# Attention loads and stores in paced pieces of about 256 KB

## The chip, the cores and the metric

The kernel runs on one core of a Trainium2 chip. The metric is the device time of one execution in microseconds; a profiled execution also gives a span from its first to its last instruction. The engines named below are TensorE (PE, with its weight loads as PEld), VectorE (DVE), ScalarE (ACT), GpSimd (POOL) and SyncE (SP), which here only issues DMAs, in the order of its queue.

## What is computed

Attention over 8 batches and 8 heads, 512 local and 32 global positions with 64 channels, then a mixture of experts on its output. Cut to what matters:

```python
s_g = scale * np.matmul(q_g, k_all.transpose(0, 1, 3, 2))        # 32 global queries see all keys
out_g = np.matmul(sm(s_g), v_all)
mask = np.abs(pos[:, None] - pos[None, :]) <= 32                 # local queries: a window and the global keys
a_l = sm(np.concatenate([s_lg, np.where(mask, s_ll, -1e9)], axis=-1))
out_l = np.matmul(a_l, np.concatenate([v_g, v_l], axis=2))
x = concat([out_g, out_l]).transpose(0, 2, 1, 3).reshape(4608, 512)
logits = x @ w_gate                                              # greedy assignment, 576 tokens to each expert
out[assigned == e] = np.maximum(x[assigned == e] @ w1[e], 0.0) @ w2[e]
```

## The kernel before

Attention runs as 40 steps, five for each batch: four local ones, each for a pair of heads (`Local`), and one for the 32 global queries of all heads (`Glob`). In the last batch the global step comes second. Tile `qk` holds the transposed queries and keys of a pair (704 KB), `vw` its values in an even and an odd arrangement: the even half comes by DMA (520 KB), the odd half by four GpSimd copies from it (`load_v`). Seven buffers of each rotate.

The order is written by hand. In loop turn i, TensorE computes the scores S of step i+2 (L169, or L248 and L256 for a global step), transposes the probabilities of step i (T, L132 or L205), and computes the outputs O of step i-1 (L143, or L223 for a global step, which reads the vw tiles of all four pairs). Transposes and small matmuls for the gate (L274, L280, L289) of earlier batches follow. VectorE masks (L122) and normalises (L149 to L154), ScalarE takes the exponential (L127) and moves T into SBUF (L266). After the last local step of a batch its output tile `xs` (1 MB) is stored to `xd` in one DMA (L157); a global step stores eight pieces of 8 KB from `xg` (L235). Routing and the experts' stage (from about 240 us) come after.

All these DMAs stand in SP's queue. At the head of a turn the loop issues loads up to four pairs ahead of the pair whose scores are due, qk in two DMAs (L75, L76) and vw in two (L84). A DMA into a buffer waits until its last readers are done, and each DMA on SP waits for the eighth before it to have landed (eight semaphores in turn); whatever stands behind it in the queue waits too.

Of the kernel before, what the change touches and what calls it, by code (L numbers as in the profile page):

```python
# [63 lines left out]
def attention(ctx, tc, A, consts, xd, ident, L, nbatch, rt=None):  # L64
# [5 lines left out]

    qk, vw, xs = {}, {}, {}

    def load_qk(b, p):
        t = ld.tile([128, QW + KW], F32, name="qk", bufs=7)
        nc.sync.dma_start(t[:, :QW], A["qk"][b, p, :, :QW])  # L75
        nc.sync.dma_start(t[:, QW:], A["qk"][b, p, :, QW:])  # L76
        qk[b, p] = t

    def load_v(b, p):
        t = ld.tile([128, 2, 2, NW // 2, D + 1], F32, name="vw", bufs=7)  # L80
        ev, od = t[:, 0], t[:, 1]
        n = NW // 2
        for h in range(2):
            nc.sync.dma_start(ev[:, h].rearrange("p w d -> p (w d)"), A["vw"][b, p, :, h * n * (D + 1):(h + 1) * n * (D + 1)])  # L84
        nc.gpsimd.tensor_copy(od[0:64], ev[64:128])  # L85
        nc.gpsimd.tensor_copy(od[64:96], ev[32:64])
        nc.gpsimd.tensor_copy(od[96:128, :, :n - 1], ev[64:96, :, 1:])
        nc.gpsimd.tensor_copy(od[96:128, :, n - 1:], ev[64:96, :, n - 1:])
        vw[b, p] = t
# [6 lines left out]
    load_qk(0, 0)  # L96
    nc.sync.dma_start(mask.rearrange("p a b -> p (a b)"), A["mask"])
    nc.sync.dma_start(ident, A["ident"])
    load_qk(0, 1)
    load_v(0, 0)  # L100
    nc.sync.dma_start(wg.rearrange("p a b -> p (a b)"), A["wg"])
    load_qk(0, 2)
    load_v(0, 1)
    nl = [3]
    warm = ac.tile([128, 128], F32, name="warm")
    nc.vector.memset(warm, 0.0)
    wt = ps.tile([128, NB, 128], F32, name="T", bufs=3)
    for _ in range(WARM):
        nc.tensor.matmul(wt[:, 0, :], warm, warm, start=True, stop=True)
    for i in range(3):  # L110
        nc.gpsimd.memset(pg[i], 0.0)

    class Local:
# [15 lines left out]
        def turn(s):  # L129
            s.t = ps.tile([128, NB, 128], F32, name="T", bufs=3)  # L130
            for c in range(NB):
                nc.tensor.transpose(s.t[:, c, :], s.p[:, c, :], ident)  # L132

        def take(s):
            s.pt = wk.tile([128, NB, 128], F32, name="pt", bufs=5)
# [2 lines left out]
        def out(s):  # L138
            b, q, h = s.b, s.q, s.h
            s.o = ps.tile([128, NB, D + 1], F32, name="O", bufs=2)  # L140
            for c in range(NB):
                for r in range(4):
                    nc.tensor.matmul(s.o[32 * r:32 * r + 32, c, :], s.pt[:, c, 32 * r:32 * r + 32],  # L143
                                     vw[b, q][:, r % 2, h, 2 * c + r // 2, :], start=True, stop=True)

        def norm(s):
            b, q, h, o = s.b, s.q, s.h, s.o
            ls = wk.tile([128, NB], F32, name="ls", bufs=4)
            nc.vector.tensor_scalar(ls, o[:, :, D], 1e-9, None, op0=ALU.add)  # L149
            nc.vector.reciprocal(ls, ls)  # L150
            if q + h == 0:
                xs[b] = wk.tile([128, NB, DM], F32, name="xs", bufs=2)
            hd = 2 * q + h
            nc.vector.tensor_tensor(xs[b][:, :, 64 * hd:64 * hd + 64], o[:, :, 0:D],  # L154
                                    ls[:, :, None].to_broadcast([128, NB, D]), op=ALU.mult)
            if q == NP - 1 and h == 1:
                nc.sync.dma_start(ap_of(xd, (b * S + SG) * DM, [[DM, 128], [128 * DM, NB], [1, DM]]), xs[b])  # L157

    def local_scores(u):
        t = qk[u[0].b, u[0].q]  # L160
        for x in u:
            x.st = ps.tile([128, NB, 128], F32, name="S", bufs=3)
        for c in range(NB):
            for r in range(4):
                j = 4 * c + r
                k0 = QW + 32 * ((3 * j + 1) // 2)
                for h in range(2):
                    e = slice(64 * h, 64 * h + 64)
                    nc.tensor.matmul(u[h].st[32 * r:32 * r + 32, c, :], t[e, 32 * j:32 * j + 32], t[e, k0:k0 + 128],  # L169
                                     start=True, stop=True)  # L170

    class Glob:
# [27 lines left out]
        def turn(s):  # L200
            s.t = []
            for lo, n in ((0, 4), (4, 2)):
                t = ps.tile([128, NB, 128], F32, name="T", bufs=3)
                for k in range(n):
                    nc.tensor.transpose(t[:, k, :], s.p[:, lo + k, :], ident)  # L205
                s.t.append(t)
                s.part(lo, n)

# [8 lines left out]
        def out(s):  # L217
            b, h = s.b, s.h
            s.o = ps.tile([128, D], F32, name="O", bufs=2)
            for k in range(6):  # L220
                for r in range(4):
                    j = 3 * k + 1 if k < 5 else 14
                    nc.tensor.matmul(s.o[32 * r:32 * r + 32, :], s.pt[:, k, 32 * r:32 * r + 32],  # L223
                                     vw[b, r][:, j % 2, h, j // 2, 0:D],
                                     start=(k == 0), stop=(k == 5))

# [11 lines left out]
    def glob_scores(u):  # L238
        b = u[0].b
        for x in u:  # L240
            x.sa = ps.tile([128, 512], F32, name="S", bufs=3)
        for x, n, k in zip(u, "ST", (3, 3)):
            x.sb = ps.tile([128, 32], F32, name=n, bufs=k)

        def small(h):
            for r in range(4):
                e = slice(64 * h, 64 * h + 64)
                nc.tensor.matmul(u[h].sb[32 * r:32 * r + 32], qk[b, r][e, SL:SL + SG], qk[b, r][e, QW + 32:QW + 64],  # L248
                                 start=True, stop=True)
        small(0)  # L250
        for r in range(4):
            for h in range(2):
                t = qk[b, r]
                e = slice(64 * h, 64 * h + 64)
                base = t[e, QW + 64:QW + 128]
                nc.tensor.matmul(u[h].sa[32 * r:32 * r + 32].rearrange("p (a b) -> p a b", b=64), t[e, SL:SL + SG],  # L256
                                 ap_of(base, 0, [list(base.ap[0]), [96, 8], [1, 64]]), start=True, stop=True)
        small(1)

# [10 lines left out]
    def gate_x(src, xt, c, spare):  # L270
        t = ps.tile([128, NB, 128], F32, name="S" if spare else "T", bufs=3 if spare else 3)
        n = src.shape[1]
        for k in range(n):
            nc.tensor.transpose(t[:, k, :], src[:, k, c * 128:(c + 1) * 128], ident)  # L274
        evac(xt[:, c, :n * 128], t[:, :n].rearrange("p a b -> p (a b)"), "x")

    def gate_m(xt, n):
        lt = ps.tile([128, 512], F32, name="T", bufs=3)
        for c in range(4):
            nc.tensor.matmul(lt[32 * c:32 * c + 32, :n * 128], wg[:, c, :], xt[:, c, :n * 128],  # L280
                             start=True, stop=True)
        ltc = wk.tile([128, 512], F32, name="ltc", bufs=2)
        evac(ltc[:, :n * 128], lt[:, :n * 128], "l")
        return ltc

    def gate_l(ltc, J, n):
        t = ps.tile([128, NB, 4, 32], F32, name="T", bufs=3)
        for k in range(n):
            nc.tensor.transpose(t[:, k].rearrange("p a b -> p (a b)"), ltc[:, k * 128:(k + 1) * 128], ident)  # L289
# [36 lines left out]
    for b in range(nbatch):  # L326
# [11 lines left out]
        else:  # L338
# [5 lines left out]
            if gl:  # L344
# [3 lines left out]
                put(s0 + 9, 0, gl[4])  # L348
                put(s0 + 10, 0, gl[5])

    first = rt.setup(slice(0, 28)) if rt else None
    LA = 2
    for i in range(-LA, ns + 1):
        if rt and i == 1:
            rt.load()
# [15 lines left out]
        if cur:  # L371
            cur[0].turn()
        if cur:
            cur[0].take()
        if cur:
            cur[1].turn()
        if cur:
            cur[1].take()
        if nx:
            nx[0].mask()  # L380
        if nx:
# [4 lines left out]
            nx[1].exp()  # L386
        if old:
            old[0].out()
        if old:
            old[0].norm()  # L390
        if old:
            old[1].out()
        if old:
            old[1].norm()
        for f in extra.get((i, 0), []):
            f()
        for f in extra.get((i, 1), []):
            f()
        for f in extra.get((i, 2), []):
            f()  # L400
        if rt and i >= ns - 1:
            for _ in range(12):
                next(first, None)
# [649 lines left out]
```

## Time and profile before

| | us |
|---|---|
| median of 3 runs (740.04 to 744.93) | 743.16 |
| the profiled execution | 743.98 |
| its span | 742.2 |
| attention and gate, to the last L289 | about 240 |
| share of the 16 DMA engines, 18 to 197 us, in SP's queue | 65.6% |

The rows of the profile are read so. A row of waits names the engine and line that was idle, what released it, the sum, the count and the longest in us. "issue" stands for a time in which the engine waited for no other engine and no DMA that the profile shows. A row of a window gives its bounds, its length, each engine's busy time with the number of instructions, the clock granted to TensorE (1.00 is full), the mean busy share of the DMA engines and GB/s. A row of the timeline gives start, length, engine, line, operation, tiles and count, with the idle time before it in brackets. DMA queue rows give the queue and kind, packets, MB and share of the 16 engines.

### The profile page before, as it was taken

What the parts mean: (1) busy time and instruction counts of PE and PEld (TensorE: products, weight loads), DVE (VectorE), ACT (ScalarE), POOL (GpSimd) and SP (SyncE); (2) the same over time, 40 slices, a digit from 0 to 9 for tenths busy, and PEclk for the clock granted to TensorE, in tenths of its full rate; (3) what the DMA queues carried; (4) which work ended last, traced back from release to release, by engine and by line L of the source; (5) the groups of instructions that cost most, each with busy time, mean ns of one, the idle gap of its engine ahead of it and who ended that gap; (6) DMA issues with size and microseconds to landing.
All of it is one profiled execution on the core that took longest, in us unless ns stands there. A gap on an engine that the chain in (4) does not pass through costs nothing.

```text
span 742.2 us, 23504 instructions
## 1 busy us (share of the span) xinstructions
PE 667.9 (90%) x9824; PEld 543.8 (73%) x9824; DVE 480.3 (65%) x1762; ACT 320.1 (43%) x867; POOL 220.2 (30%) x247
## 2 busy tenths in 40 slices
PE   7788889888697259999999999999999999999997
PEld 6566657666474159778878978978877987988985
DVE  3586767677576788867676777775876865551410
ACT  5676766767481024334334334343342423541420
POOL 4833553553520040052043034034024025312002
PEclk8999999999898569999999999999999999999999
DMA  9665864876622052081072063044035044522001
GB/s 343 262 210 169 293 223 152 284 256 185 221 93 76 1 181 108 1 284 65 2 263 85 2 241 108 2 165 169 16 128 206 17 172 155 195 68 94 15 15 46
DMA packets 37034, 103.36 MB, mean 139 GB/s; under 512 B 7232, under 2 KB 7488, under 8 KB 32832
## 3 DMA queue, kind: packets, MB, share of 16 engines
q0 software_dynamic: 10240, 51.39, 19.8%
q1 hardware_dynamic: 26688, 50.48, 19.7%
q8 instruction: 77, 1.26, 0.7%
q14 instruction: 29, 0.24, 0.1%
HBM read 84.02 MB, written 17.83 MB: 137 GB/s over the span
## 4 chain that ended last, share of the span: by engine, by line
PE 77%; DVE 10%; issue 6%; DMA 4%; ACT 2%; SPq 0%; POOLq 0%; POOL 0%; DVEq 0%; ACTq 0%
PE Y L931 22%; PE H L903 21%; PE S L169 6%; PE T L132 5%; PE O L143 4%; PE R L513 4%; PE H L775 2%; DVE r_G L445 2%; PE T L274 2%; DVE w2l L445 2%; PE T L205 2%; PE Y L921 2%; PE O L223 2%; DMA qk<-in_qk_dram 1%; PE T L280 1%
## 5 line engine op out<-in xcount | busy, mean ns | idle before, releaser
L903 PE MATMUL H<-xh,w1h 128*128 128x272 f32 x512 | 151.4, 296 | 1.8 <-DVE hl L445 1.4
L903 PE MATMUL H<-xh,w1l 128*128 128x272 f32 x512 | 149.9, 293 | 0.0
L903 PE MATMUL H<-xl,w1h 128*128 128x272 f32 x512 | 149.9, 293 | 0.0
L905 ACT ACTIVATE hh<-H 128x272 fp32r<-128x272 f32 x128 | 50.9, 398 | 130.2 <-PE H L903 125.7
L931 PE MATMUL Y<-w2h,hh 128*128 128x512 f32 x256 | 103.9, 406 | 0.0
L931 PE MATMUL Y<-w2l,hh 128*128 128x512 f32 x256 | 102.7, 401 | 0.0
L931 PE MATMUL Y<-w2h,hl 128*128 128x512 f32 x256 | 102.4, 400 | 0.0
L903 PEld LDWEIGHTS H<-xh,w1h 128*128 128x128 f32 x512 | 96.5, 188 | 5.2 <-DVE hl L445 2.4
L903 PEld LDWEIGHTS H<-xl,w1h 128*128 128x128 f32 x512 | 96.5, 188 | 0.6
L903 PEld LDWEIGHTS H<-xh,w1l 128*128 128x128 f32 x512 | 96.4, 188 | 0.3
L122 DVE CUSTOM_DVE_ANT_0 p<-S,mask 128x128 f32<-128x128 f32 x256 | 56.7, 286 | 40.9 <-PE S L169 40.8
L127 ACT ACTIVATE p<-p,nm 128x128 f32<-128x128 f32 x256 | 78.0, 397 | 7.5 <-DVE nm L122 7.5
L782 POOL DMA_INDIRECT out_dram<-y,idx x40 | 39.7, 992 | 136.1 <-ACT y L873 79.2
L736 POOL DMA_INDIRECT w1r<-in_w_dram,widx x16 | 15.6, 977 | 208.4 <-DVE r_a L445 126.6
L445 DVE SCALAR_TENSOR_TENSOR hl<-H,hh 128x272 fp32r<-128x272 f32 x128 | 54.4, 433 | 23.5 <-ACT h L907 12.7
L445 DVE TENSOR_TENSOR w2l<-w2r,w2h 128x512 fp32r<-128x512 f32 x64 | 43.1, 687 | 37.5 <-ACT w2h L752 37.1
L85 POOL COPY vw<-vw 64x1040 f32<-64x1040 f32 x32 | 33.5, 1047 | 109.3 <-DMA vw<-in_vw_dram 90.9
L873 ACT ACTIVATE y<-Y 128x512 f32<-128x512 f32 (+1 forms) x40 | 23.2, 594 | 92.3 <-PE Y L931 70.6
L169 PE MATMUL S<-qk 64*32 64x128 f32 x2048 | 47.3, 300 | 15.5 <-issue 12.0
L931 PEld LDWEIGHTS Y<-w2h,hh 128*128 128x128 f32 x256 | 48.2, 188 | 15.8 <-issue 5.9
L266 ACT ACTIVATE pt<-T 128x512 f32<-128x512 f32 x64 | 35.6, 596 | 55.4 <-PE T L132 55.1
L752 ACT ACTIVATE w1h<-w1r 128x512 fp32r<-128x512 f32 x64 | 36.4, 622 | 49.9 <-DVE L L445 30.3
(169 smaller groups left out, 1250.0 us busy)
## 6 DMA issues: line engine op xcount, KB each, us to landing
vw<-in_vw_dram SPq DMA_DIRECT2D x64, 260.0 KB, 5.9
qk<-in_qk_dram SPq DMA_DIRECT2D x32, 432.0 KB, 5.8
qk<-in_qk_dram SPq DMA_DIRECT2D x32, 272.0 KB, 5.1
xd<-xs SPq DMA_DIRECT2D x8, 1024.0 KB, 8.2
xd<-xg SPq DMA_DIRECT2D x64, 8.0 KB, 3.4
xg<-xd,idx POOLq DMA_INDIRECT x40, 3.5
out_dram<-y,idx POOLq DMA_INDIRECT x40, 2.7
cf<-in_cf_dram SPq DMA_DIRECT2D x1, 512.0 KB, 6.7
```

The source lines that it names most:

```text
L85: nc.gpsimd.tensor_copy(od[0:64], ev[64:128])
L122: nc.vector.tensor_tensor_reduce(s.p[:, c, :], s.st[:, c, :], mask[:, c, :], -SCALE, BIG, ALU.add, ALU.min, s.nm[:, c:c + 1])
L127: nc.scalar.activation(s.p[:, c, :], s.p[:, c, :], AF.Exp, bias=s.nm[:, c:c + 1], scale=-1.0)
L132: nc.tensor.transpose(s.t[:, c, :], s.p[:, c, :], ident)
L169: nc.tensor.matmul(u[h].st[32 * r:32 * r + 32, c, :], t[e, 32 * j:32 * j + 32], t[e, k0:k0 + 128], start=True, stop=True)
L266: nc.scalar.activation(dst, src, AF.Copy)
L445: return op(*args, **kw)
L752: nc.scalar.activation(hi, raw, AF.Copy)
L782: nc.gpsimd.indirect_dma_start(out=out, out_offset=bass.IndirectOffsetOnAxis(ap=rt.idx[ph][:n, t:t + 1], axis=0), in_=y[:n], in_offset=None)
L903: nc.tensor.matmul(p, w[d][:, fs], x[:, d, q], start=(d + k == 0), stop=(d + k == 5))
L905: nc.scalar.activation(hh[:, f, q], p, AF.Relu)
L931: nc.tensor.matmul(p, h[:, f, q], w[f], start=(f + k == 0), stop=(f + k == 9))
```

## The change

Every TensorE call of the attention stage goes through a wrapper that remembers the last instruction. `paced` issues a DMA with a dependency on that instruction, so that SP issues it when TensorE has done it. `load_qk`, `load_v` and the new `store_x` are generators: a qk tile comes in three pieces, a vw tile in two, and an xs tile is stored in four (the last batch's in one DMA, as before). Up front a plan gives each load a time in steps, three before its need or earlier, 1.25 steps apart at most. Six times a turn `pump` issues at most one piece that is due; a load starts only if one of its seven buffers has been given back by program order.

```diff
+    def paced(dst, src):
+        d = nc.sync.dma_start(dst, src)
+        if pe.last is not None:
+            tc.add_manual_dep(d.ins, pe.last.ins.name,
+                              mybir.DependencyInfo(mybir.DependencyClass.Sync, mybir.DependencyReason.DATA), reason="pace")
+
     def load_qk(b, p):
         t = ld.tile([128, QW + KW], F32, name="qk", bufs=7)
-        nc.sync.dma_start(t[:, :QW], A["qk"][b, p, :, :QW])
-        nc.sync.dma_start(t[:, QW:], A["qk"][b, p, :, QW:])
         qk[b, p] = t
+        paced(t[:, :QW], A["qk"][b, p, :, :QW])
+        yield
+        for k in range(2):
+            w = KW // 2
+            paced(t[:, QW + k * w:QW + k * w + w], A["qk"][b, p, :, QW + k * w:QW + k * w + w])
+            if k == 0:
+                yield
...
+    def store_x(b):
+        for k in range(NB):
+            r = b * S + SG + 128 * k
+            paced(xd[r:r + 128, :], xs[b][:, k])
+            yield
...
+    for f, n0, lead, t0 in ((load_qk, 3, 3.0, -LA), (load_v, 2, 3.0, -LA + 0.6)):
+        late = [need[f, b, p] - lead for b, p in P]
+        for n in range(len(P) - 2, -1, -1):
+            late[n] = min(late[n], late[n + 1] - 0.8)
+        t = t0
+        for n in range(n0, len(P)):
+            t = max(t0, min(late[n], t))
+            plan.append((t, f, P[n]))
+            t += 1.25
...
+    def piece(t):
+        for k, (t1, g) in enumerate(loading):
+            if t1 <= t:
+                if next(g, g) is g:
+                    loading.pop(k)
+                else:
+                    loading[k] = (max(t, t1) + 0.25, g)
+                return True
+        for k, (t1, f, bp) in enumerate(plan):
+            if t1 > t:
+                break
+            if live[f] < room[f]:
+                live[f] += 1
+                plan.pop(k)
+                g = f(*bp)
+                next(g)
+                loading.append((t + 0.25, g))
+                return True
...
         if nx:
-            p = nx[0].b * NP + nx[0].last
-            while nl[0] < len(P) and nl[0] <= p + 4:
-                load_qk(*P[nl[0]])
-                load_v(*P[nl[0] - 1])
-                nl[0] += 1
-                if nl[0] == len(P):
-                    load_v(*P[-1])
-        if nx:
             (local_scores if isinstance(nx[0], Local) else glob_scores)(nx)
+            used(load_qk, nx)
+        pump(i + 0.00)
         if cur:
             cur[0].turn()
         if cur:
             cur[0].take()
+        pump(i + 0.14)
...
```

What this does to SP's queue, first in the middle of the stage, around the store of the first batch's xs. "DMAHW" is the semaphore of an earlier DMA, "PE", "DVE" and "Pool" stand for waits on those engines. Before:

```order
L75 DMA qk<-in_qk_dram 128x544 [waits DMAHW6_49]
L76 DMA qk<-in_qk_dram 128x864 [waits DMAHW7_49]
L84 DMA vw<-in_vw_dram 128x520 [waits DMAHW0_49,PE_49,Pool_49]
L84 DMA vw<-in_vw_dram 128x520 [waits DMAHW1_49]
L157 DMA xd<-xs 128x4x512 [waits DMAHW2_49,DVE_49]
L75 DMA qk<-in_qk_dram 128x544 [waits DMAHW3_49]
L76 DMA qk<-in_qk_dram 128x864 [waits DMAHW4_49]
```

And now:

```order
L90 DMA vw<-in_vw_dram 128x520 [waits DMAHW1_49,PE_49]
L90 DMA qk<-in_qk_dram 128x544 [waits DMAHW2_49,PE_49]
L90 DMA qk<-in_qk_dram 128x432 [waits DMAHW3_49,PE_49]
L90 DMA xd<-xs 128x512 [waits DMAHW4_49,DVE_49]
L90 DMA qk<-in_qk_dram 128x432 [waits DMAHW5_49,PE_49]
L90 DMA xd<-xs 128x512 [waits DMAHW6_49,PE_49]
L90 DMA xd<-xs 128x512 [waits DMAHW7_49,PE_49]
```

The pieces of loads and stores stand in turn, and nearly each waits for TensorE by itself, where before a row of DMAs followed one wait. SP has 265 entries for 213.

Second, SP's queue at the end of the stage, from the last vw tile on (x2 is two DMAs in a row). Before:

```order
L76 DMA qk<-in_qk_dram 128x864
L84 DMA vw<-in_vw_dram 128x520 x4
L157 DMA xd<-xs 128x4x512
L235 DMA xd<-xg 32x64 x16
L312 DMA gx<-xd 32x512 x4
```

And now:

```order
L90 DMA qk<-in_qk_dram 128x432
L90 DMA vw<-in_vw_dram 128x520 x2
L90 DMA xd<-xs 128x512 x3
L276 DMA xd<-xg 32x64 x8
L90 DMA xd<-xs 128x512
L90 DMA vw<-in_vw_dram 128x520 x2
L276 DMA xd<-xg 32x64 x8
L353 DMA gx<-xd 32x512 x4
```

The last pair's vw has moved behind batch 6's xs store and its eight xg stores. On TensorE, VectorE, ScalarE and GpSimd the instructions and their order are the same as before.

More of the change, by code (lines that the diff above doesn't have):

```diff
@@ L71, in attention, with __init__, __getattr__, issue @@
     qk, vw, xs = {}, {}, {}
+    class Engine:
+        def __init__(s, eng):
+            s.eng, s.last = eng, None
+        def __getattr__(s, name):
+            op = getattr(s.eng, name)
+            def issue(*args, **kw):
+                s.last = op(*args, **kw)
+                return s.last
+            return issue
+    pe = Engine(nc.tensor)
+    def paced(dst, src):
[3 more added lines that the diff above has]
+                              mybir.DependencyInfo(mybir.DependencyClass.Sync, mybir.DependencyReason.DATA), reason="pace")
     def load_qk(b, p):
         t = ld.tile([128, QW + KW], F32, name="qk", bufs=7)
-        nc.sync.dma_start(t[:, :QW], A["qk"][b, p, :, :QW])
-        nc.sync.dma_start(t[:, QW:], A["qk"][b, p, :, QW:])
         qk[b, p] = t
+        paced(t[:, :QW], A["qk"][b, p, :, :QW])
[5 more added lines that the diff above has]
+                yield
     def load_v(b, p):
         t = ld.tile([128, 2, 2, NW // 2, D + 1], F32, name="vw", bufs=7)
+        vw[b, p] = t
         ev, od = t[:, 0], t[:, 1]
@@ L83, in load_v @@
         for h in range(2):
-            nc.sync.dma_start(ev[:, h].rearrange("p w d -> p (w d)"), A["vw"][b, p, :, h * n * (D + 1):(h + 1) * n * (D + 1)])
+            w = n * (D + 1)
+            paced(ev[:, h].rearrange("p w d -> p (w d)"), A["vw"][b, p, :, h * w:h * w + w])
+            if h == 0:
+                yield
         nc.gpsimd.tensor_copy(od[0:64], ev[64:128])
@@ L94, in attention, with now @@
     P = [(b, p) for b in range(nbatch) for p in range(NP)]
-    load_qk(0, 0)
+    def now(*loads):
+        for x in loads:
+            for _ in x:
+                pass
+    now(load_qk(0, 0))
     nc.sync.dma_start(mask.rearrange("p a b -> p (a b)"), A["mask"])
     nc.sync.dma_start(ident, A["ident"])
-    load_qk(0, 1)
-    load_v(0, 0)
+    now(load_qk(0, 1), load_v(0, 0))
     nc.sync.dma_start(wg.rearrange("p a b -> p (a b)"), A["wg"])
-    load_qk(0, 2)
-    load_v(0, 1)
-    nl = [3]
+    now(load_qk(0, 2), load_v(0, 1))
     warm = ac.tile([128, 128], F32, name="warm")
@@ L131, in turn @@
             for c in range(NB):
-                nc.tensor.transpose(s.t[:, c, :], s.p[:, c, :], ident)
+                pe.transpose(s.t[:, c, :], s.p[:, c, :], ident)
         def take(s):
@@ L156, in norm @@
             if q == NP - 1 and h == 1:
-                nc.sync.dma_start(ap_of(xd, (b * S + SG) * DM, [[DM, 128], [128 * DM, NB], [1, DM]]), xs[b])
+                if b < nbatch - 1:
+                    work.append(store_x(b))
+                else:
+                    nc.sync.dma_start(ap_of(xd, (b * S + SG) * DM, [[DM, 128], [128 * DM, NB], [1, DM]]), xs[b])
     def local_scores(u):
@@ L204, in turn @@
                 for k in range(n):
-                    nc.tensor.transpose(t[:, k, :], s.p[:, lo + k, :], ident)
+                    pe.transpose(t[:, k, :], s.p[:, lo + k, :], ident)
                 s.t.append(t)
@@ L273, in gate_x @@
         for k in range(n):
-            nc.tensor.transpose(t[:, k, :], src[:, k, c * 128:(c + 1) * 128], ident)
+            pe.transpose(t[:, k, :], src[:, k, c * 128:(c + 1) * 128], ident)
         evac(xt[:, c, :n * 128], t[:, :n].rearrange("p a b -> p (a b)"), "x")
@@ L288, in gate_l @@
         for k in range(n):
-            nc.tensor.transpose(t[:, k].rearrange("p a b -> p (a b)"), ltc[:, k * 128:(k + 1) * 128], ident)
+            pe.transpose(t[:, k].rearrange("p a b -> p (a b)"), ltc[:, k * 128:(k + 1) * 128], ident)
         nc.vector.tensor_reduce(L[:, J:J + n, :], t[:, :n, :, 0:8].rearrange("p k c e -> p k e c"),
@@ L349, in attention, with used, pump @@
                 put(s0 + 10, 0, gl[5])
+    LA = 2
+    need, left = {}, {}
+    for i, u in enumerate(steps):
+        for q in [u[0].q] if isinstance(u[0], Local) else range(NP):
+            for f, t in ((load_qk, i - LA), (load_v, i + 1)):
+                k = f, u[0].b, q
+                need[k] = min(t, need.get(k, t))
+                left[k] = left.get(k, 0) + 1
+    live = {load_qk: 3, load_v: 2}
+    room = {load_qk: 7, load_v: 7}
+    plan = []
+    for f, n0, lead, t0 in ((load_qk, 3, 3.0, -LA), (load_v, 2, 3.0, -LA + 0.6)):
[7 more added lines that the diff above has]
+            t += 1.25
+    plan.sort(key=lambda x: x[0])
+    work, loading = [], []
+    def used(f, u):
+        for q in [u[0].q] if isinstance(u[0], Local) else range(NP):
+            left[f, u[0].b, q] -= 1
+            live[f] -= left[f, u[0].b, q] == 0
+    def piece(t):
[3 more added lines that the diff above has]
+                    loading.pop(k)
+                else:
+                    loading[k] = (max(t, t1) + 0.25, g)
[10 more added lines that the diff above has]
+                return True
+    def pump(t):
+        for _ in range(1):
+            while work:
+                loading.append((t, work.pop()))
+            piece(t)
     first = rt.setup(slice(0, 28)) if rt else None
-    LA = 2
     for i in range(-LA, ns + 1):
@@ L378, in attention @@
             cur[1].take()
+        pump(i + 0.29)
         if nx:
@@ L388, in attention @@
             old[0].out()
+        pump(i + 0.43)
         if old:
@@ L392, in attention @@
             old[1].out()
+            used(load_v, old)
         if old:
             old[1].norm()
+        pump(i + 0.57)
         for f in extra.get((i, 0), []):
@@ L400, in attention @@
             f()
+        pump(i + 0.71)
         if rt and i >= ns - 1:
```

16 lines of the change are left out of this document (8 added, 8 removed).

## The prediction

> **What bounds the kernel now.** I read the page first, then the chain of waits, then the waits of TensorE alone, then tables by window. From the page:
>
> ```profile
> span 742.2 us, 23504 instructions
> PE 667.9 (90%) x9824; PEld 543.8 (73%) x9824; DVE 480.3 (65%) x1762; ACT 320.1 (43%) x867; POOL 220.2 (30%) x247
> PE 77%; DVE 10%; issue 6%; DMA 4%; ACT 2%; SPq 0%; POOLq 0%; POOL 0%; DVEq 0%; ACTq 0%
> q8 instruction: 77, 1.26, 0.7%
> ```
>
> TensorE carries the chain. The 6% called issue are waits for nothing that another engine does. That is some 44 us; the next view finds 27.9 of them in the attention stage (the first 230 us), the only stage whose code changes. The last row gives a reason: 77 transfers of kind "instruction" moved 1.26 MB, 16 KB each, and TensorE has 2 x 9824 instructions, 255 for each transfer. So it lives on blocks of some 255 instructions. TensorE's own waits on issue between 18 and 197 us:
>
> ```profile
> PE S L169 <- issue: 12.0, 12, 2.4
> PE O L143 <- issue: 7.6, 6, 2.2
> PE T L274 <- issue: 2.6, 2, 1.8
> PE O L223 <- issue: 2.5, 4, 1.3
> PE T L132 <- issue: 1.7, 2, 1.3
> PE T L248 <- issue: 1.5, 1, 1.5
> ```
>
> That is 27.9 us in 27 waits, and they stand one block apart. The table by window, cut from the end of one wait to the end of the next (columns: length, busy time and instructions of PE, PEld, DVE, ACT, POOL, then granted clock, DMA share, GB/s):
>
> ```profile
> 67.28:70.98 3.70, 3.14 (x127) 2.61 (x127) 2.66 (x22) 2.62 (x8) 2.08 (x3) 1.00 0.04 16
> 70.98:75.91 4.93, 4.22 (x129) 3.43 (x128) 3.87 (x23) 2.90 (x10) 1.57 (x2) 1.00 0.85 256
> 75.91:82.29 6.38, 4.55 (x127) 3.24 (x127) 4.63 (x17) 5.00 (x20) 4.73 (x7) 1.00 1.04 393
> 96.27:99.98 3.71, 3.15 (x133) 2.62 (x127) 2.73 (x16) 2.77 (x9) 0.00 (x0) 1.00 0.32 80
> 99.98:105.88 5.90, 4.37 (x128) 3.05 (x128) 5.03 (x27) 3.41 (x10) 3.27 (x4) 1.00 0.97 289
> 105.88:111.79 5.91, 4.08 (x127) 3.14 (x127) 2.65 (x10) 3.46 (x14) 3.28 (x4) 1.00 0.96 362
> 121.95:125.39 3.44, 3.21 (x127) 2.68 (x127) 2.16 (x19) 2.49 (x8) 2.57 (x3) 1.00 0.06 22
> ```
>
> Each row holds about 254 instructions (PE plus PEld). With the DMA engines nearly free (share 0.04 to 0.32) the wait, length less PE busy, is 0.56, 0.56 and 0.23 us; with them full (0.85 to 1.04) it is 0.71, 1.83, 1.53 and 1.83. The block's own transfer tells why. DMA rows of four pieces, 67.28 to 68.65 and 68.65 to 70.98, then 75.91 to 80.05 and 80.05 to 82.29:
>
> ```profile
> q1 hardware_dynamic: 13, 0.03, 6.4%
> ```
> ```profile
> q8 instruction: 1, 0.02, 2.5%
> ```
> ```profile
> q1 hardware_dynamic: 817, 1.63, 103.5%
> ```
> ```profile
> q8 instruction: 1, 0.02, 2.7%
> ```
>
> In the free stretch the instruction packet starts 1.4 us after the block boundary, in the full one 4.1 us after it, and lasts 1 us in both (2.5% of 16 engines x 2.33 us, 2.7% of 16 x 2.24). So what differs is how long it stands behind the loads. The loads stand there in heaps because SP's queue is held:
>
> ```profile
> SPq L84 <- PE O L223: 66.8, 7, 15.5
> ```
>
> Seven times SP waits for the last reader of a vw buffer, up to 15.5 us, and then issues all that is due at once.
>
> The Trainium skill, "Runtime: NRT & Kernel Launch", section "Instruction fetch mechanics", says blocks of 256 instructions are fetched while the block before runs and the cost of a boundary is mostly hidden. The block size agrees with the 254 here; "hidden" does not agree with 27.9 us of waits, and the rival called "hidden" below shows what it would make of the time.
>
> **The waits cost twice.** TensorE's timeline around one wait:
>
> ```profile
> 79.08 1.12 PE L143 MATMUL O<-vw,pt 128*32 128x65 f32 x64
> 82.30 0.90 PE L274 MATMUL T<-ident,xs 128*128 128x128 f32 x3 [1.84 <-issue]
> 83.13 1.96 PE L169 MATMUL S<-qk 64*32 64x128 f32 x64
> 87.97 1.16 PE L169 MATMUL S<-qk 64*32 64x128 f32 x64
> ```
>
> After the wait of 1.84 us the same 64 matmuls take 1.96 instead of 1.16 us. The table of such stretches shows the granted clock (first and last of six; the four between stand at 82.35, 113.0, 136.9 and 194.9, all at 0.50 or 0.51):
>
> ```profile
> 27.60:31.00 3.40, 3.10 (x59) 2.69 (x60) 1.04 (x9) 0.04 (x1) 3.26 (x5) 0.51 0.91 349
> 201.70:205.10 3.40, 3.14 (x27) 2.45 (x16) 1.91 (x6) 0.87 (x2) 2.87 (x3) 0.50 0.02 5
> ```
>
> 3.4 us at half clock lose 1.7 us of work.
>
> **The change, part by part** (against the profiled execution, 743.98 us, of which 742.2 are span; the median of the runs is 743.16).
>
> *Even loads.* A qk or vw tile comes in 3 and 2 pieces, an xs store in 4, each behind another TensorE instruction, at most six pieces a step. Over an undisturbed batch DVE, ACT and POOL have room:
>
> ```profile
> 103.48:131.01 27.53, 23.63 (x720) 17.93 (x712) 18.98 (x108) 18.24 (x59) 12.80 (x16) 0.94 0.65 220
> ```
>
> The share of 0.65 is now made of full and empty stretches; afterwards it should be 0.65 to 0.75 throughout, with one or two pieces queued, not eight transfers. What a block waits there no row shows exactly. Bounds: from below, the three free rows, mean 0.45 us, for the 27 in 37 blocks that waited at all (the others held slower instructions), 12.2 us; even less, 5 us, if shorter waits shift the boundaries well; from above the 27.9 of today or, if an even load is worse, more (a rival). I take 12.2 plus 1.5 for the one block in each batch that meets the pieces heaped behind the eight small stores, nearer to the free rows because the backlog is what differs: 13.7. Gain 14.2.
>
> *Clock.* Five of the six half-clock stretches follow issue waits: 5 x 1.7 = 8.5. I keep one (1.7), and give back 1.3 because shorter blocks hide less of a fetch: gain 5.5.
>
> *The late qk of the last batch.* Its global scores need all four qk tiles and wait for one:
>
> ```profile
> 200.72 0.22 PE L248 MATMUL S<-qk 64*32 64x32 f32 x2 [2.54 <-DMA qk<-in_qk_dram]
> ```
>
> With the half-clock stretch behind it, 2.5 + 1.7 = 4.2. After the change these pieces go out one to two steps ahead, the last behind the scores of the step before; 0.7 us of waiting remains, I estimate from that one piece. Gain 3.5.
>
> *A new wait at vw of the last pair.* Its buffer comes free when the outputs of batch 6's global queries have been read; today its two loads go out at once, and GpSimd's four copies end just as batch 7's global outputs begin:
>
> ```profile
> 209.46 1.55 PE L223 MATMUL O<-vw,pgt 128*32 128x64 f32 x96
> 211.00 0.28 DVE L233 TENSOR_SCALAR xg<-O,gm 128x64 f32<-128x64 f32 x1
> 211.05 0.81 SPq L84 DMA_DIRECT2D vw<-in_vw_dram  x2
> 215.93 1.05 POOL L85 COPY vw<-vw 64x1040 f32<-64x1040 f32 x1 [10.43 <-PE O L143]
> 219.00 0.29 POOL L88 COPY vw<-vw 32x130 f32<-32x130 f32 x1
> 219.37 1.55 PE L223 MATMUL O<-vw,pgt 128*32 128x64 f32 x96
> L235 SPq DMA_DIRECT2D xd<-xg x64: 302/388/1847, 51.0 to 224.7; - x64
> ```
> ```profile
> DMA to landing us min/median/max: 2.6/5.9/10.1
> ```
>
> There is no slack: 219.29 against 219.37. Afterwards SP first issues the eight xg stores of batch 6 (from 211.3, when xg is there, 8 x 0.42 = 3.4 us), one piece of xs, then the two vw pieces: the second at 215.9, landed 2.6 us later (the least of all) to 4.4 (today: second issue at 211.5, first copy at 215.93), copies 3.4 us: 221.9 to 223.7. TensorE waits 2.5 to 4.3 us, and waits over 1.8 us have had a half-clock stretch behind them. I take 3.7 + 1.3 = 5.0, between 0 (if SP gets past the stores sooner) and 6.0.
>
> *What costs nothing.* More DMA instructions on SP (265 rows for 213): about 24 large and 8 small issues of some 0.4 us in a batch of 27.5 us. Loads in mid-stage go out two or more steps (some 10 us) ahead of need, above the median landing of 5.9; if that cover went, TensorE would wait for qk as at 200.72. Order and number of instructions on the compute engines stay as they were, and the experts' stage is untouched.
>
> Sum: -14.2 - 5.5 - 3.5 + 5.0 = -18.2, so 743.98 - 18.2 = 725.8, **726 us**.
>
> **Rivals.**
> *Better:* blocks wait nearly as in the free rows (8 us left, gain 19.9), no half-clock stretch remains of five (6.8 after the same give-back of 1.7), the qk wait goes (4.2), the late vw costs 3.4 without its clock: -27.5, 716.5 us. For it: rows at share 0.32 already look like 0.04. Against: the load will be double that.
> *Partly:* the pieces pile up behind the eight small stores, which hold SP for 8 us in the row below, and 20 us of waits remain; less clock is won (4.0): -7.9 - 4.0 - 3.5 + 5.0 = -10.4, 733.6 us. Against: today's 8 us are mostly waits for heaped loads to land.
>
> ```profile
> 51.01 8.00 SPq L235 DMA_DIRECT2D xd<-xg  x8
> ```
>
> *Hidden:* the waits do not come from the loads. They and the clock stay; 3.5 gained, 5.0 lost: 745.5 us. Against it stand the seven window rows. The page of the Trainium skill named above speaks for this rival.
> *Slower:* the load spread evenly makes every block wait a middling time. Between 3.70 us from boundary to boundary at share 0.04 and 6.38 at 1.04, share 0.65 gives 5.3. Blocks without waits take (181 - 27.9)/37 = 4.1 us (181 us from 19 to 200): 37 x 1.2 = 44 us of waits for 27.9, +16, less 8.5 clock and 3.5, plus 5: 753 us. It decides if the even load keeps boundaries over 4.9 us apart (4.1 + 27.9/37). Against it: at share 0.32 the row shows no more delay than at 0.04, so the delay comes from the backlog.
>
> **How the numbers follow.** Chances: forecast 0.48 (its own range 719 to 731), better 0.20, partly 0.17, hidden 0.07, slower 0.08. About 1% (7.4 us) is what a measurement of this kernel can tell from no change, so faster means under 735.7: forecast, better, and about half of partly, 0.77; within 1% the rest of partly and hidden, 0.16; slower 0.07. The range reaches from a little under better to past partly, 714 to 741, and leaves out hidden, slower and some of better's tail.
>
> **What would show it.** Issue waits of TensorE before 200 us near 14 us; granted clock at 0.5 once or not at all between 30 and 190 us; DMA digits in attention level instead of 9 and 0; a TensorE wait of 3 to 4 us at L223's successor in the last batch, behind a vw copy; the experts' stage as long as before. It is wrong if the block waits grow in number to one per block, or if TensorE waits for qk or vw in mid-stage.

## The result and the profile after

| | before | after |
|---|---|---|
| median of 20 runs each, in turn | 743.07 us (739.61 to 750.03) | 739.29 us (731.46 to 745.52) |
| ratio, with its 95% interval | | 0.9939 [0.9917, 0.9962] |
| the profiled execution | 743.98 us | 735.21 us |

The change gains 4.5 us by the ratio, a quarter of the 18.2 that were forecast. The profiled executions are 8.8 us apart, but that of after lies 4.1 us below its own median and that of before 0.9 above. So a second profile of each is used further down. One run of after, the 745.52 us, was in a slower state and is left out of the ratio.

From the page of after, the span, the engines' busy time, the clock and DMA lines over 40 slices, and the largest group of the experts' stage:

```profile
span 733.4 us, 23676 instructions
PE 660.2 (90%) x9824; PEld 537.3 (73%) x9824; DVE 478.8 (65%) x1762; ACT 320.3 (44%) x867; POOL 220.0 (30%) x247
...
PEclk8999999999997589999999999999999999999999
DMA  9875876887321070261081082063035055521001
...
L997 PE MATMUL H<-xh,w1h 128*128 128x272 f32 x512 | 151.4, 296 | 1.9 <-DVE hl L539 1.4
```

The DMA digits of the attention stage (the first ten) are 5 to 9, before 4 to 9: fuller, hardly more level. How far apart attention ends is read from the first of the H matmuls. Line groups of after and of before (first and last start):

```profile
L997 PE MATMUL H<-xh,w1h x512: 282/288/397, 270.4 to 703.0; 128*128 128x272 f32 x171
```
```profile
L903 PE MATMUL H<-xh,w1h x512: 282/288/396, 279.5 to 711.8; 128*128 128x272 f32 x171
```

In these two executions the experts start 9.1 us earlier and then take as long as before (733.4 - 270.4 = 463.0 us, 742.2 - 279.5 = 462.7). All of the difference lies ahead of them.

TensorE's waits of after between 18 and 230 us, those on issue, vw and qk (L83 is the wrapper through which every matmul of the stage now goes):

```profile
PE S L83 <- issue: 9.4, 6, 2.0
PE O L83 <- issue: 9.1, 10, 1.8
PE O L83 <- POOL vw L118: 4.3, 1, 4.3
...
PE S L83 <- DMA qk<-in_qk_dram: 2.9, 1, 2.9
PE T L83 <- issue: 1.3, 2, 0.9
```

Block waits (TensorE's waits on issue) fell from 27.9 us in 27 waits to 19.8 us in 18, not to 13.7. The wait for qk stayed (2.5 before). The wait for the last pair's vw has come as forecast. Two rows of the timeline of TensorE place both in the last batch:

```profile
186.76 1.86 PE L83 MATMUL S<-qk 64*32 64x32 f32 x16 [2.88 <-DMA qk<-in_qk_dram]
...
209.85 2.66 PE L83 MATMUL O<-vw,pgt 128*32 128x64 f32 x89 [4.34 <-POOL vw L118]
```

And the stretches at half clock up to 220 us, by window, are two where before had six (the second follows the wait for vw):

```profile
58.80:62.20 3.40, 3.40 (x35) 2.91 (x36) 1.78 (x16) 1.67 (x5) 1.88 (x3) 0.50 0.31 83
209.00:212.40 3.40, 2.55 (x93) 2.55 (x97) 0.67 (x4) 0.00 (x0) 1.03 (x2) 0.50 0.02 5
```

SP's queue shows one thing that is not even. Its timeline of after around a batch's eight xg stores in mid-stage, and in the last but one batch:

```profile
93.57 5.29 SPq L276 DMA_DIRECT2D xd<-xg  x8
98.97 0.36 SPq L90 DMA_DIRECT2D vw<-in_vw_dram  x1
99.43 0.38 SPq L90 DMA_DIRECT2D xd<-xs  x1
99.93 0.36 SPq L90 DMA_DIRECT2D vw<-in_vw_dram  x1
...
197.11 4.16 SPq L276 DMA_DIRECT2D xd<-xg  x8
201.37 0.37 SPq L90 DMA_DIRECT2D xd<-xs  x1
201.84 0.87 SPq L90 DMA_DIRECT2D vw<-in_vw_dram  x2
```

SP is held for 5.3 us, and then the pieces that fell due meanwhile follow each other every half microsecond. The even pace is broken once in each batch. Whether that is where TensorE then waits is another question, taken up below.

### The profile page after: what moved, and what is told of

Its sections match the earlier page's. It is cut to its first block, busy times and chain, and to the rows that moved or that the text cites. A ratio compares the mean times of both kernels' runs of the same rounds, so it can differ in the third digit from the quotient of the medians.

```text
span 733.4 us, 23676 instructions
## 1 busy us (share of the span) xinstructions
PE 660.2 (90%) x9824; PEld 537.3 (73%) x9824; DVE 478.8 (65%) x1762; ACT 320.3 (44%) x867; POOL 220.0 (30%) x247
## 4 chain that ended last, share of the span: by engine, by line
PE 46%; DVE 4%; DMA 2%; issue 2%; ACT 1%; POOLq 0%; DVEq 0%; ACTq 0%
PE Y L1025 21%; PE H L997 18%; PE R L607 3%; PE H L869 2%; DVE w2l L539 2%; PE Y L1015 2%; DMA w1r<-in_w_dram,widx 1%; DVE r_G L539 1%; ACT w2h L846 1%; DVE hl L539 0%; DVE r_pm L539 0%; DMA xg<-xd,idx 0%; PE Y L1031 0%; DMA out_dram<-y,idx 0%; DVE w1l L539 0%
## 5 line engine op out<-in xcount | busy, mean ns | idle before, releaser
L83 PE MATMUL S<-qk 64*32 64x128 f32 (+2 forms) x2240 | 55.7, 298 | 18.2 <-issue 9.4
L967 ACT ACTIVATE y<-Y 128x512 f32<-128x512 f32 (+1 forms) x40 | 23.2, 594 | 91.9 <-PE Y L1025 70.6
L83 PEld LDWEIGHTS S<-qk 64*32 64x32 f32 x2240 | 34.5, 108 | 34.5 <-issue 18.5
```

The costliest lines, as they stand in the source:

```text
L83: s.last = op(*args, **kw)
L967: nc.scalar.activation(y[:n], p[:n], AF.Copy)
```

## The experiments

They ran on other chips, on which before takes 750.9 to 752.2 us, so they are compared by their ratio to before on the same chip. On that footing the change itself gave 0.994 [0.9914, 0.9966] again. "Block waits" are TensorE's waits on issue between 18 and 197 us in one profiled execution.

| kernel | ratio to before | median, us | block waits, us |
|---|---|---|---|
| before, profiled again | | 751.86 (one run) | 26.2 |
| after, again | 0.994 [0.9914, 0.9966] | 747.83 | 20.1 |
| xg stores paced too | 0.999 [0.9959, 1.0022] | 752.58 | 20.6 |
| last vw ahead of the xg stores | 0.9825 [0.9784, 0.9866] | 739.64 | 21.8 |
| split only, no pace | 0.9936 [0.9906, 0.9966] | 747.35 | 22.0 |
| pace only, whole tiles | 0.9905 [0.9872, 0.9938] | 744.61 | 23.2 |
| loads of seven pairs only | 0.9501 [0.9459, 0.9542] | 712.87 | 5.4 |
| last batch put in order | 0.9813 [0.9775, 0.985] | 738.36 | 19.9 |
| the same, two xg stores for eight | 0.9705 [0.9666, 0.9745] | 729.00 | 15.0 |
| last batch, at most four pieces out | 1.0106 [1.0063, 1.0149] | 758.59 | 10.7 |
| last batch, vw of seven pairs only | 0.965 [0.9613, 0.9687] | 724.95 | 11.9 |
| after, two xg stores for eight | 0.9802 [0.9772, 0.9832] | 734.99 | 18.3 |
| before, two xg stores for eight | 0.9967 [0.9947, 0.9988] | 747.35 | 26.8 |

**Are the eight stores in the way, or the pace?** First, the xg stores of batches 0 to 5 take their turn among the paced pieces, four at a time.

```diff
+    def store_g(b, h, xg):
+        for r in range(4):
+            paced(ap_of(xd, b * S * DM + (2 * r + h) * D, [[DM, SG], [1, D]]), xg[32 * r:32 * r + 32, :])
+        yield
...
+            if b < nbatch - 2:
+                work.append(store_g(b, h, xg))
+            else:
...
```

> The eight small xg stores of batches 0 to 5 are handed to the pump, four at a time, so that they no longer stand as eight in a row in SP's queue and no longer make it wait for VectorE. Theory A (the gain was cut because SP is held at these stores once a batch and then issues all that has become due in a heap): TensorE's issue waits from 18 to 190 us fall from 19.6 us in the changed kernel to about 14, the time falls by 4 to 6 us against the changed kernel, so to 9 to 11 us under the kernel before. Theory B (the load is too high by itself, some 70% of the DMA engines in the dense turns, and an even flow delays a fetch as well): issue waits stay at 18 to 21 us and the time at 4 to 5 us under the kernel before.

The ratio of 0.999 can't be told from no gain. Block waits stayed at 20.6 us, and TensorE waited nine times for qk, 8.6 us in all. There are still eight DMAs to issue, and now they take the turns of loads, which come late. SP still waited 5.1 us for xg between 18 and 200 us, 5.6 in the first profile of after, so the edit hardly removed that wait either. It can't say whether the stores in a row or their number matter.

**The last pair's vw.** It is loaded as soon as batch 6's global outputs have been read, ahead of that batch's xg stores.

```diff
+            if isinstance(old[0], Glob) and old[0].b == nbatch - 2:
+                now(load_v(*P[-1]))
...
+            while held:
+                held.pop(0)()
```

> The last pair's vw tile is loaded at once when its buffer comes free, ahead of batch 6's xg stores. If the wait of 4.3 us for GpSimd's copies in the last batch, and the half clock behind it, are lost time, then the wait goes and the time falls by 4 to 6 us against the changed kernel, to 9 to 11 us under the kernel before. If another wait takes its place (VectorE and the gate at the end of the stage are late anyway), the time stays within 1.5 us of the changed kernel's.

SP's timeline shows the two loads in front:

```profile
202.58 0.83 SPq L90 DMA_DIRECT2D vw<-in_vw_dram  x2
203.50 4.55 SPq L277 DMA_DIRECT2D xd<-xg  x8
```

No wait for vw was left, and the ratio went from 0.994 to 0.9825, some 8 us. The order of this queue had cost that much. Block waits did not fall with it (21.8 us).

**Only splitting, without a pace.** This is before, with its qk in three pieces and xs stored in four.

```diff
-        nc.sync.dma_start(t[:, QW:], A["qk"][b, p, :, QW:])
+        for k in range(2):
+            w = KW // 2
+            nc.sync.dma_start(t[:, QW + k * w:QW + k * w + w], A["qk"][b, p, :, QW + k * w:QW + k * w + w])
...
```

> The kernel before with the smaller pieces alone (qk in three, xs stores in four), at their old places and without waits on TensorE. If the size of a transfer matters (a fetch stands behind one transfer), the issue waits fall from 27 to about 20 us and the time by 5 to 8 us against the kernel before. If the number of bytes queued matters and not how they are cut, the issue waits stay at 25 to 29 us and the time within 2 us of the kernel before.

It gained 4.8 us by the ratio, as much as the whole change. The transfers still leave in heaps and block waits are 22.0 us. Some 5 us can thus be had without a pace; but the change also pays for its late loads, so this does not show that the pace is worth nothing.

**Only the pace, with whole tiles.** After, with qk in two and xs in one DMA, at the planned times.

```diff
         paced(t[:, :QW], A["qk"][b, p, :, :QW])
+        paced(t[:, QW:], A["qk"][b, p, :, QW:])
         yield
-        for k in range(2):
...
```

> The changed kernel with the plan's times, but each tile goes out whole at its time (qk in two transfers, vw in two, an xs store in one). If the gain comes from spreading the tiles over the steps, issue waits are 19 to 22 us and the time as the changed kernel's, 3 to 5 us under the kernel before. If it comes from the pieces within a tile, issue waits are back at 25 us or more and the time is within 2 us of the kernel before, or above it by the late vw.

The ratio is 0.9905, no worse than that of the change with its pieces. The wait for vw was 1.1 us here and that for qk 0.5, beside block waits of 23.2. So neither expectation was met, and its 7 us by the ratio come only in part from block waits (26.2 to 27.9 in before): it is also spared most of the late data that the change pays for. Splitting and pacing each give about what both give together. That is no proof that their gains don't add, since the late data differ too.

**Do the loads cause the block waits at all?** After, with loads for the first seven pairs only; later pairs read the first batch's tiles, so the output is that of other data, and GpSimd's copies of these tiles are left out too.

```diff
+    for n in range(7, len(P)):
+        alias[P[n]] = P[n % 4]
...
+    plan = [x for x in plan if P.index(x[2]) < 7]
```

> The changed kernel with loads for the first seven head pairs only; the later pairs compute on the tiles of the first batch (so the output is that of other data), while all stores stay. Theory fetch behind loads: with hardly any load traffic after 20 us the blocks of TensorE instructions arrive as in the free rows, issue waits from 25 to 190 us are 5 to 12 us, nothing waits for qk or vw, and the time falls by 15 to 25 us against the changed kernel. Rival (the waits at the block boundaries are TensorE's own and not the loads'): issue waits stay near 20 us and only the waits for qk and vw go, 5 to 9 us under the changed kernel.

TensorE's waits on issue, 18 to 197 us, and a window without loads:

```profile
PE O L89 <- issue: 2.6, 3, 1.9
PE S L89 <- issue: 2.4, 5, 1.1
...
PE T L89 <- issue: 0.4, 1, 0.4
```
```profile
25.00:185.00 160.00, 154.51 (x5093) 119.10 (x5097) 134.05 (x778) 130.28 (x412) 11.38 (x15) 1.00 0.19 65
```

With the DMA share at 0.19 the waits are 5.4 us, the clock is full throughout, and the kernel is 35 us faster than after on the same chip, where 15 to 25 were expected. That is what the loads and GpSimd's copies cost in all. The Trainium skill, "Runtime: NRT & Kernel Launch", section "Instruction fetch mechanics", calls the boundary of a block mostly hidden: that agrees with this run, and not with the kernel as it stands.

**After and before once more,** unchanged, in this group.

> The changed kernel once more, on the same chip as the others of this group: again 3 to 6 us under the kernel before, with a wait of about 4 us for GpSimd's copies at the last batch's global outputs. If its time under the kernel before is 8 us or more here, the chips differ in what they make of the change.

> The kernel before once more, for a second profile on the chip of this group. Its issue waits between 18 and 190 us should again be 25 to 29 us with five or more stretches of half clock in the attention stage; if they differ by more than 4 us between two profiles, single profiles are too uncertain for differences of a few us and the timed ratios decide.

TensorE's waits of after in this execution, 18 to 230 us:

```profile
PE S L83 <- issue: 12.2, 9, 2.5
PE S L83 <- DMA qk<-in_qk_dram: 6.7, 5, 3.0
PE O L83 <- issue: 6.2, 8, 1.7
PE O L83 <- POOL vw L118: 5.2, 1, 5.2
PE T L83 <- issue: 1.7, 1, 1.7
```

and one of its now six stretches at half clock:

```profile
193.20:196.60 3.40, 3.37 (x27) 1.34 (x28) 0.15 (x1) 0.00 (x0) 3.27 (x4) 0.50 0.47 173
```

The block waits repeat (20.1 for 19.8, before 26.2 for 27.9). The clock does not: after has six stretches up to 220 us for two (20.5 us in all for 6.8), before seven for six (27.3 us for 20.5, one of them 6.8 us long). And four of the five waits for qk are in mid-stage:

```profile
137.17 0.77 PE L83 MATMUL S<-qk 64*32 64x128 f32 x28 [1.06 <-DMA qk<-in_qk_dram]
...
164.01 0.66 PE L83 MATMUL S<-qk 64*32 64x128 f32 x28 [1.81 <-DMA qk<-in_qk_dram]
...
193.23 2.34 PE L83 MATMUL S<-qk 64*32 64x32 f32 x16 [2.96 <-DMA qk<-in_qk_dram]
```

They stand 27 to 29 us, one batch, apart: from 137 us on, a qk tile is late once in each batch.

**The last batch put in order.** As with the last vw first, and the other vw tiles of the last batch planned 1.5 steps later, so that qk goes ahead of them.

```diff
+    plan = [(t + 1.5 if f is load_v and bp[0] == nbatch - 1 else t, f, bp) for t, f, bp in plan]
+    plan.sort(key=lambda x: x[0])
```

> As the run with the last vw tile first, and the other vw tiles of the last batch are planned 1.5 steps later, so that they do not stand between the pieces of its qk tiles. If the qk wait of 2.7 to 2.9 us before the last batch's global scores comes from vw pieces ahead of qk in SP's queue, it falls to 1 us or less and the time is 2 to 4 us below that run (about 15 us under the kernel before). If it comes from the buffer that comes free only one step before, the wait and the time stay within 1.5 us.

The wait for qk went (2.7 to 0.4 us); the ratio of 0.9813 can't be told from 0.9825. The late qk alone is worth little here.

**Two xg stores for eight.** On top of that, a head group's four stores become one DMA with a pattern of 4 x 32 x 64: two issues for each batch instead of eight, of the same bytes.

```diff
-                for r in range(4):
-                    nc.sync.dma_start(ap_of(xd, b * S * DM + (2 * r + h) * D, [[DM, SG], [1, D]]),
-                                      xg[32 * r:32 * r + 32, :])
+                nc.sync.dma_start(ap_of(xd, b * S * DM + h * D, [[2 * D, 4], [DM, SG], [1, D]]), xg)
```

> As the last-batch run, but the four xg stores of a head are one DMA of the same bytes, so that a batch has two of them in SP's queue and not eight. Theory A (SP is held some 5 us a batch at these stores and then issues a heap): issue waits from 25 to 190 us fall from 17.4 us to 13 or less and the time by 3 to 6 us against that run, to 17 to 20 us under the kernel before. Theory B (the load is high by itself): issue waits 16 to 20 us, time 12 to 15 us under the kernel before.

SP's timeline at the place where it was held for 5.3 us, and TensorE's waits from 18 to 197 us:

```profile
89.29 1.34 SPq L276 DMA_DIRECT2D xd<-xg  x2
90.74 0.41 SPq L90 DMA_DIRECT2D vw<-in_vw_dram  x1
```
```profile
PE O L83 <- issue: 7.1, 9, 1.6
PE S L83 <- issue: 6.5, 7, 1.6
PE T L83 <- issue: 1.4, 2, 1.1
...
PE O L83 <- POOL vw L118: 0.9, 1, 0.9
```

A hold of 1.3 us for 5.3, block waits of 15.0 us for the 19.9 of the run before, no wait for qk among these rows, no half clock between 18 and 200 us, and a ratio of 0.9705, 21.9 us below before. It beats both kernels and is the best of the study. The same stretch in before, then in after, then here, by window:

```profile
22.00:197.00 175.00, 146.36 (x4516) 111.32 (x4511) 122.95 (x697) 115.12 (x363) 87.18 (x107) 0.95 0.66 224
```
```profile
22.00:197.00 175.00, 150.31 (x4808) 113.92 (x4800) 128.35 (x733) 122.81 (x390) 93.22 (x115) 0.99 0.73 238
```
```profile
22.00:197.00 175.00, 156.63 (x5103) 119.84 (x5095) 136.77 (x782) 130.66 (x413) 96.66 (x119) 1.00 0.77 243
```

TensorE gets through 4516, 4808 and 5103 matmuls in the same 175 us, while the DMA engines are busier each time. The Trainium skill, "DMA: Bandwidth & Descriptors", section "Rules for kernel authors", advises to join many small transfers into a large one, since below 64 KB they are mostly overhead. The trace agrees, and says where the overhead lies here: in SP's queue, 5.29 us for eight and 1.34 for two.

**A tighter limit on what is queued.** As the last batch put in order, and each piece also waits until the fourth piece before it has landed (the queue's own limit is eight).

```diff
+        queue.append(d)
+        if len(queue) > 4:
+            tc.add_manual_dep(d.ins, queue[-5].ins.name, ..., reason="few")
```

> As the last-batch run, but a piece also waits until the fourth piece before it has landed, so that four pieces (1 MB) and not eight transfers can stand in the DMA queues. Theory C (a fetch stands behind what is queued, so the backlog sets its delay): issue waits from 25 to 190 us fall from 17.4 us to 12 or less, blocks with a delay over 1.5 us nearly vanish, and the time falls by 3 to 8 us if no load comes late, to 17 to 22 us under the kernel before. Theory B (share of the time in which the DMA engines are busy sets it, whatever stands behind): issue waits 16 to 20 us and the time 12 to 15 us under the kernel before, or worse by late loads.

TensorE's waits, 18 to 197 us, and its worst wait for qk:

```profile
PE S L83 <- DMA qk<-in_qk_dram: 14.6, 9, 5.2
PE O L83 <- issue: 5.2, 6, 1.8
PE S L83 <- issue: 3.4, 4, 1.2
PE T L83 <- issue: 2.1, 2, 1.4
```
```profile
143.41 1.21 PE L83 MATMUL S<-qk 64*32 64x128 f32 x28 [5.15 <-DMA qk<-in_qk_dram]
```

With fewer pieces in flight the block waits are 10.7 us, near the 13.7 forecast. That fits the backlog as their cause, but does not show it alone. In this trace none of the eight blocks within which TensorE stood still for over 0.5 us for something else is followed by a block wait, so the waits for qk also take the place of some block waits. The loads no longer keep up, TensorE waits 14.6 us for qk, and the kernel is 1.1% slower than before.

**Without vw's traffic.** As the last batch put in order, with vw loaded and copied for the first seven pairs only; later pairs take the first batch's values, so the output is that of other data.

```diff
+    plan = [x for x in plan if x[1] is load_qk or P.index(x[2]) < 7]
```

> As the last-batch run, without the vw loads (and GpSimd copies) of all pairs after the seventh, which use the values of the first batch (so the output is that of other data). 42% of the load bytes go. Between the 17.4 us of issue waits with all loads and 2.7 us with none: if waits follow the share of busy DMA time, 9 to 12 us and a time about 10 to 16 us below the last-batch run; if only heaps matter, which are now shorter, 7 us or less and 15 to 22 us below it.

Block waits fell to 11.9 us and the ratio from 0.9813 to 0.965, 12 us. Between all loads (about 20 us of waits) and none (5.4) the waits fall with the amount of traffic. Both numbers lie where the expectation had them if the share of busy DMA time decides, not the heaps. Against that share as the only cause stands the row of the merged stores above: 15.0 us of waits at a share of 0.77, when after had about 20 at 0.73. Which of the two delays a block, share or backlog, is not settled.

**The stores alone, in after and in before.** The same merged stores as the only edit.

> The changed kernel with nothing else altered but the eight xg stores of a batch as two DMAs of the same bytes. If the eight entries in SP's queue are the one cause behind the shortfall (heaped pieces, the late qk and the late vw of the last batch), the time is 16 to 22 us under the kernel before, issue waits from 25 to 190 us 12 to 14 us, and the wait for GpSimd's copies in the last batch falls from 4.3 to 5.2 us to under 2. If moving the vw tile and replanning the last batch were needed as well, the time is 8 to 13 us under it.

> The kernel before with the eight xg stores of a batch as two DMAs and nothing else altered. If these stores matter only because paced pieces stand behind them, the time is within 3 us of the kernel before and issue waits from 18 to 197 us stay at 24 to 28 us. If the stores cost the kernel before as much (8 us or more), the gain of the run with one xg store is theirs and not the pacing's.

In after the ratio went from 0.994 to 0.9802, some 10 us, with waits of 0.6 us for qk and, in the last batch,

```profile
PE O L83 <- POOL vw L118: 1.3, 1, 1.3
```

for vw, where the change had 4.3. Its block waits, from 18 to 197 us, are

```profile
PE S L83 <- issue: 8.6, 7, 2.0
PE O L83 <- issue: 7.5, 8, 2.2
PE T L83 <- issue: 2.2, 2, 2.0
```

That is 18.3 us in 17 waits, with about 20 in 18 before the edit; 16.4 of them lie between 25 and 190 us, where 12 to 14 were expected. The time is 15 us under that of before by the ratio and 16 by the medians, at the edge of the 16 to 22 expected. So what the eight stores cost in after is mostly late data: the waits for qk and vw fell from 9.6 us, the mean of two profiles, to 1.9, the block waits by less than 2. In before the same edit gave 0.9967, 2.5 us by the ratio. So eight stores cost little in a queue that goes in heaps anyway, and four times as much in one that is meant to go evenly.

## Why the prediction was wrong

**Right: what bounds the stage.** TensorE lives on blocks of instructions whose transfer stands behind the loads. The run without loads (block waits of 5.4 us, 19.8 and 20.1 in after) and that without vw's (11.9) show that the loads make the waits, and the rival "hidden" falls with them. "Slower" falls as well: an even load does not make every block wait. The low end of the bounds, 5 us where waits nearly vanish, was met at a DMA share of 0.19.

**Wrong in size: the block waits, -14.2.** The profiles give -8.1 in the first pair and, over two of each (before 27.9 and 26.9, after 19.8 and 20.1, between 18 and 230 us), -7.5. The step that failed is "I take 12.2 plus 1.5", and in it the first term: 27 waits of 0.45 us each, as in rows with the DMA engines nearly free. After has 18 waits in both profiles, and they last 1.1 us each, as long as those of before (27.9 us in 27). Fewer blocks wait, but under an even load a wait is not that of a free row. The "one or two pieces queued" of the prediction did not come about. From the page of after a load piece takes 4.6 to 4.9 us from issue to landing and an xs piece 3.5; with 24 pieces in a batch of 27.5 us this makes some four under way at a time, an estimate. In the traces the packet that brings a block starts on average 2.3 and 2.2 us after the boundary in the two profiles of before, 1.8 in both of after and 1.0 in the run without loads. (Boundaries without a wait are placed by counting 254 instructions.) It starts later than 3 us for 12 of 36 and 10 of 36 blocks before, for 3 of 34 and 2 of 36 after. The change took away the long delays and left middling ones. What an even load of this size does to a block, by its share or by the pieces under way, stays open.

The second term, "plus 1.5 for the one block in each batch that meets the pieces heaped behind the eight small stores", is the smaller miss. Joining the stores took less than 2 us off the block waits in after and 4.9 with the last batch in order, one execution each, and 18.3 and 15.0 us were left. Nor do the waits stand behind the stores: of the 19.8 and 20.1 us, 7.0 and 9.5 end within 15 us of the first xg store of a batch, and these stretches are half of the time. The longest in the first profile, 2.02 us, ends 23 us after one. The rival "partly" had 20 us of waits, right to 0.2, but for this heap as the reason, so that number is luck in the main. It was argued down because today's 8 us of holding were thought to be mostly waits for loads to land; SP is held 4.2 to 5.3 us in the first profile of after even so.

**Wrong: the late qk, -3.5.** It was to shrink to 0.7 us. It is 2.9 and 6.7 us in the two profiles (2.5 and 2.7 before). That "these pieces go out one to two steps ahead" was not enough. What the prediction listed under "what costs nothing", the loads in mid-stage, cost 3.8 us in the second profile, with waits at 137 and 164 us, and none in the first. With two stores for eight the waits for qk are 0.6 us in all, so most of this comes from the hold in SP's queue.

**Right in kind, too small: the late vw, +5.0.** The order in SP's queue, the eight stores in front and the wait of 2.5 to 4.3 us were read off correctly: 4.34 and 5.19 us were measured, the first with the half-clock stretch that was allowed for. Taking it away gained about 8 us, three more than forecast. Where these three come from was not taken apart.

**Not settled: the clock, -5.5.** Up to 220 us, before has 20.5 and 27.3 us at half clock in its two profiles, after 6.8 and 20.5. Half of that is lost work, so the means differ by -5.1, where the forecast has -5.9 with the clock parts of the late qk and the late vw. That it comes so close may be chance: single executions of one kernel differ by more, and after's runs spread over 10 us even without the one left out of the ratio. That "waits over 1.8 us have had a half-clock stretch behind them" did not hold in before itself: after the wait of 2.23 us that ends at 21.71 the clock is 1.00 up to 27.60. Nor does any run show the 1.3 us that were given back because shorter blocks hide less of a fetch.

Summed over the means of two profiles: -7.5 for blocks, +2.2 for qk (4.8 for 2.6), +4.8 for vw, -5.1 for the clock, -5.6 us in all. The experts start 5.1 us earlier on the same mean, and the ratio gives 4.5. Split the same way, the forecast was -14.2, -1.8, +3.7 and -5.9. Of the 12.6 us between the two sums, 6.7 lie in the block waits and 4.0 in the late qk. The split rests on two executions each and is no closer than that.

**What the forecast was a forecast of.** Without the late vw its sum was -23.2 us. The version with two stores for eight and the last batch in order has hardly a wait for vw (0.9 us) and a short hold, and gains 21.9. Its parts are not those of the forecast: its block waits are 15.0 us, not 13.7, and between 18 and 200 us no half clock is left where one stretch was kept. The prediction priced an even load; the change did not make one. The eight stores were in the order of SP's queue, and in the rows quoted, from the start.

## What to carry to other kernels

When loads are given a pace, look through the queue that issues them for anything that does not follow the pace: eight small stores of 8 KB made data late, and joining them gave more than twice what the change itself gave. Do not price a wait under load from rows without load: these waits became fewer, not shorter. A limit on the transfers in flight went with shorter block waits and made data late; both sides must be priced (10.7 us of block waits against 14.6 of waits for qk). A single profile gives a sum of stalls to a few microseconds only, so an effect below 1% is taken from runs and ratios.

## What was not expected of the hardware

Smaller transfers were not worse: cutting qk's 432 KB into two of 216 and xs's 1 MB into four of 256, with nothing else changed, gave 0.9936.

Half clock follows short waits, but not each of them. In after, the stretch from 58.80 us on stands behind this wait on issue:

```profile
58.56 0.47 PE L83 MATMUL S<-qk 64*32 64x128 f32 x3 [1.93 <-issue]
```

while the waits of 2.02 us at 141.28 and of 2.88 us at 186.76 have none behind them. The second profile of after, with a wait of the same size at 193.23, had a stretch behind it. So the length of a wait does not decide it alone, and the clock term changes much from one execution to the next. What else decides it was not looked for.

The chips differ by one per cent: before takes 743.1 us on one and 751 to 752 on three others. In the second profile of before, from its line groups,

```profile
L903 PE MATMUL H<-xh,w1h x512: 282/288/428, 281.9 to 719.6; 128*128 128x272 f32 x171
```

the experts' stage takes 468.1 us (750.0 of span less 281.9) instead of 462.7, so most of the difference between chips lies where nothing was changed. Its cause was not looked for.
